# First block of a routed expert layer: order of its downs and place of its counting and weight loads

## The chip, the core and the metric

The kernel runs on one core of a Trainium2 chip. The metric is the device time of one execution in microseconds (us); it is given as the median of several runs.

PE is TensorE (matmul), PEld its weight load, DVE VectorE, ACT ScalarE, POOL GpSimd and SP SyncE. SPq, ACTq and POOLq are the sequencers of these engines, which wait, branch and issue DMAs.

## What is computed

Attention over keys and values that are pooled by eight, then a layer of eight experts of which each token takes one (4608 tokens of 512 numbers, 1024 hidden columns):

```python
k_p = k.reshape(B, H, Sp, pool, D).mean(axis=3)
v_p = v.reshape(B, H, Sp, pool, D).mean(axis=3)
...
x = np.ascontiguousarray(attn_out.transpose(0, 2, 1, 3)).reshape(B * S, H * D)
...
logits = x @ w_gate
expert_idx = np.argmax(logits, axis=1)
...
    h = np.maximum(x_sorted[lo:hi] @ w1[e], 0.0)
    y_sorted[lo:hi] = h @ w2[e]
y = y_sorted[inv_perm]
return (gate_w[:, None] * y).astype(np.float32)
```

## The kernel before

The attention runs as 36 units (NU = 36) of 128 tokens in a loop that is unrolled when the program is built. Its tokens are routed in seven groups. A token's row goes to the tensor in DRAM named x_by_expert, sorted by expert, with an indirect DMA that POOL issues, one for each unit (scatter, L709). The expert layer then takes blocks of 256 sorted tokens. Every fp32 operand is used as a pair of fp16 numbers, high and low, so that each product is three matmuls.

The loop over blocks (For_i, L1316) runs 21 times. The **first block** of expert 0 stands ahead of it, unrolled, and overlaps the last units and the last routing. Its work on PE is eight "ups", f = 0 to 7 (L1007 to L1009, 12 matmuls each), and four "downs" (finish(0, j, half), L1084, 12 matmuls each): j is the half of the tokens, half is the half of the hidden columns. Three of the ups stand inside units 33 to 35 (UPAT), and the rest behind the units. The ups' results lie in four PSUM tiles of two columns f each; relu_hi(k) on ACT (L1075) and relu_lo(k) on DVE (L1078) turn tile k into the high and low fp16 operands of the downs. So downs with half = 0 need k = 0 and 1, and downs with half = 1 need k = 2 and 3. In the trace the downs of j = 1 write the tile pq, those of j = 0 the tile po.

Between the ups two steps of the routing are put:

- counted() (L1104) multiplies the counts per expert (c16) by ones on PE, and rank() runs the ranks of the last group. DVE makes from it the comparison lt and the counts, and SP issues two DMAs of zero rows (L1117).
- ended() (L1138) sums lt on PE, runs the rest of the last group's routing on DVE, and has POOL issue the scatters that are left and three DMAs of zero rows (L1122).

DVE then works out a table of the blocks (table(), L1156 to L1182, 27 small operations). tables() turns it on PE (L1185), DVE writes it as integers into tabs (L1186), and SP reads from tabs which rows the next blocks need. It then issues load_x(1) into the tile qt (L1231) and load_x(2) into vb. The block of iteration 0 is expert 0's second: its rows xT come by a DMA transpose (trans, L929) that SP issues after split_lo (L918), and arrive() (L933) copies them on DVE after tabs. POOL splits the rows of load_x(1) (split_early, L911 and L912), passes their identities on, and enters the loop. In iteration 0 ACT splits x (L915) and then, with DVE, the weights of expert 1 into fp16 pairs (part(), L116 on ACT and L118 on DVE). PE's next block waits for that.

The weights of expert 1 come as four loads of 1 MB from DRAM (wload, L102), all issued by SP, in the units that W1AT names: two halves of w1 at units 28 and 31, then the second half of w2 at unit 32 and the first half at unit 35. A place of NU + k in W1AT would move a load to wlate(k), which issues it behind the units; before the change no load is there.

The engines take their instructions in the order in which the program is written. There is no scheduler between.

Of the kernel before, what the change touches and what calls it, by code (L numbers as in the profile page):

```python
# [22 lines left out]
CW = 73  # L23
WARM = 80
CS = 78
W1AT = (28, 31, 35, 32)
UPAT = (33, 34, 35)
HS = (0, 1, 3, 5, 5)
SLOTS = ((0, 2), (0, 3), (0, 3), (0, 3), (2, 3))
# [3 lines left out]
def kernel(  # L33
# [10 lines left out]
    nc = tc.nc  # L44
# [43 lines left out]
            src = src[e:e + 1] if isinstance(e, int) else src[ds(e, 1)]  # L88
            nc.sync.dma_start(dst, src.rearrange("e p c f -> p (e c) f"))

    def wload(e, i, stage=0):

        lo, hi = (i, i + 1) if isinstance(i, int) else i
        a, n = lo % 4, hi - lo
        s1, s2 = ST[stage]
        if lo < 4:
            src, dst = w1d, s1[a // 2][:, a % 2:a % 2 + n, :]
        else:
            src, dst = w2d, s2[a // 2][:, 2 * (a % 2):2 * (a % 2 + n), :]
            a, n = 2 * a, 2 * n  # L100
        src = src[e:e + 1, :, a:a + n, :] if isinstance(e, int) else src[ds(e, 1), :, a:a + n, :]
        nc.sync.dma_start(dst, src.rearrange("e p c f -> p (e c) f"))  # L102

    last_pool = []

# [120 lines left out]
    def row(x):  # L226

        return x[..., 0:ID].rearrange("p j (h x) -> p j h x", x=HW)[..., 0:D]

    def col(h):  # L230
        return h.rearrange("p j (h x) -> p j h x", x=D)
# [36 lines left out]
    for c in range(5):  # L268
        src = w_gate.rearrange("(h d) e -> d h e", d=D)[:, HS[c]:HS[c] + 3, :]
# [489 lines left out]
    def pooled(n, b):  # L759
        KVS[n, b] = work.tile([128, 5, D], F32, name=n, bufs=2)  # L760
        return kv[(2 * b + (n == "vp")) % 3], KVS[n, b]
# [11 lines left out]
    src, vp = pooled("vp", 0)  # L773
# [86 lines left out]
    for g in range(NPAIR):  # L860
        u0 = 9 * g
        e, o = 2 * g, 2 * g + 1
# [51 lines left out]
    def split_hi():  # L914
        nc.scalar.activation(col(xh[:, :, 0]), row(xg), AF.Copy)  # L915
# [57 lines left out]

    for j, at in enumerate(W1AT):
        if at < NU:
# [26 lines left out]
    def up(s, f, n):  # L1002
        dst = pH[f // 2][:, (f % 2) * BLK:(f % 2) * BLK + n]
        c = slice(f * 128, (f + 1) * 128)
        for d in range(DC):
            wh, wl = W1[s][0][:, d, c], W1[s][1][:, d, c]
            nc.tensor.matmul(dst, wh, xT[:, d, 0:n], start=(d == 0), stop=False)  # L1007
            nc.tensor.matmul(dst, wh, xT[:, DC + d, 0:n], start=False, stop=False)  # L1008
            nc.tensor.matmul(dst, wl, xT[:, d, 0:n], start=False, stop=(d == DC - 1))  # L1009
# [58 lines left out]
    def pair(x, k, n):  # L1068
        return x[:, 2 * k:2 * k + 2, 0:n]

    def ups_of(k, n):
        return pH[k].rearrange("p (f t) -> p f t", f=2)[:, :, 0:n]

    def relu_hi(k, n=BLK):
        nc.scalar.activation(pair(hT[0], k, n), ups_of(k, n), AF.Relu)  # L1075
# [26 lines left out]
    def counted():  # L1102
        pc = pq["pc"] = psA.tile([128, 512], F32, name="pq", bufs=2)
        nc.tensor.matmul(pc[:, 0:E], ones, c16, start=True, stop=True)  # L1104
        rank()
        lt = pq["lt"] = work.tile([128, E], F16, name="lt")
        V.tensor_tensor(lt, pc[:, 0:E], thr, op=OP.is_gt)
        V.tensor_copy(pads, pc[0:1, 0:E])
        for x in range(2):
            h = slice(64 * x, 64 * x + 64)  # L1110
            V.tensor_scalar(padi[h], pc[h, 0:E].rearrange("p (c x) -> p c x", x=2)[:, :, x], pio[h], None, op0=OP.add)
        pcs = pq["pcs"] = work.tile([128, E], F32, name="pcs")
        V.tensor_copy(pcs, pc[:, 0:E])
        for e in range(n0 + n1):
            eng, et = ((nc.sync, ENG.SP), (nc.scalar, ENG.Activation))[e >= n0]
            r = nc.values_load(pads[0:1, e:e + 1], engines=[et], min_val=e * SEG, max_val=e * SEG + SEG - 128)
            padded.append((e, sent(eng.dma_start(xs[ds(r, 64), :], zpad[0:64]))))  # L1117
# [16 lines left out]
    def ended():  # L1134
        pe = psA.tile([128, 512], F32, name="pq", bufs=2)
        end = pq["end"] = pe[:, 0:E]
        for j in range(E):
            nc.tensor.matmul(end[:, j:E], ones, pq["lt"][:, 0:E - j], start=(j == 0), stop=False,  # L1138
                             skip_group_check=True)
        for f in back:  # L1140
            f()
        scatters()
        flush()
        pad_rest()

    def wlate(k):
        for j, at in enumerate(W1AT):
            if at == NU + k:
                wload(1, (2 * j, 2 * j + 2))

    def table():
        end, pcs = pq["end"], pq["pcs"]
# [31 lines left out]
    def tables(pt):  # L1184
        nc.tensor.transpose(pt[0:NK, 0:128], tf[:, 0:NK], ident)  # L1185
        V.tensor_copy(tabs, pt[0:NK, 0:NT])  # L1186
# [3 lines left out]
    for f in range(FC):  # L1190
        if f >= len(UPAT):
            up(0, f, BLK)
        if f + 1 == 5:
            counted()
        if f + 1 == 6:
            ended()
        if f in (1, 3):
            relu_hi(f // 2)
    split_hi()
    for k in (2, 3):  # L1200
        relu_hi(k)
# [10 lines left out]
    W2[1] = [x.rearrange("p (c f) -> p c f", c=FC) for x in views[2:]]  # L1212
    pY.append(psA.tile([128, 512], F32, name="pq", bufs=2))
    pH[3] = psA.tile([128, 512], F32, name="pq", bufs=2)
    for j, half in ((1, 0), (1, 1), (0, 0), (0, 1)):
        if (j, half) == (0, 1):
            tables(pH[3])
            arrive()
        finish(0, j, half)
# [39 lines left out]
        given.append(st)  # L1259

    load_x(1, xg2)
    wlate(1)
    with tc.If(ok2 < 1):
        load_x(0)
        split_x()
# [100 lines left out]
```

## Time and profile before

| what | value |
|---|---|
| time, median of 3 runs | 610.75 us (606.24, 610.75, 615.33) |
| the profiled execution's own time | 615.37 us |
| its span in the profile | 613.4 us |
| PE busy | 570.7 us, 93% of the span |
| DVE, ACT, POOL busy | 51%, 48%, 44% of the span |
| granted TensorE clock, mean | 0.989 of full speed |

Times in the rows below count from the start of the span, which is 613.4 us; 2 us of the execution's own time lie around it. Units and routing end at about 190 us, the first block at about 209 us, and the loop fills the rest. A row's bracket gives the idle time of the engine before it and what ended it; "remote" is a semaphore event to which the profile finds no instruction, and "issue" is a wait to which it finds none.

### The profile page before, as it was taken

The numbers are of one execution on the slowest core, as the hardware profiler recorded it, in microseconds if no ns is written. First come the engines' busy times: TensorE is split into PE (matmuls) and PEld (weight loads), VectorE is DVE, ScalarE is ACT, GpSimd is POOL, SyncE is SP. The second block draws the span as 40 slices with busy tenths as digits, with TensorE's granted clock in tenths as the row PEclk, the third lists the DMA queues.
The fourth block names the chain that finished last, engine by engine and source line by source line (L and its number), as shares of the span: only waits on it lengthen the run. The fifth ranks groups of instructions, "written<-read, shape, count | busy, mean of one in ns | idle before, by whom it ended". The sixth has DMA issues, their size and how long they took to land.

```text
span 613.4 us, 15789 instructions
## 1 busy us (share of the span) xinstructions
PE 570.7 (93%) x4725; PEld 419.2 (68%) x4726; DVE 312.0 (51%) x625; ACT 291.6 (48%) x648; POOL 269.3 (44%) x524
## 2 busy tenths in 40 slices
PE   7888889999887998988999999999999999999995
PEld 6777879887765556645767756767656667567663
DVE  6677897987865355125762782213622471122122
ACT  2677789899941154125653672223522452222122
POOL 5799598997976243211432321122311132211212
PEclk9899999999989899999999999999999999999998
DMA  8997898885496557963986779143332324321200
GB/s 236 315 316 228 264 311 252 277 255 197 137 352 162 166 92 262 380 102 95 309 273 201 205 240 336 56 107 81 78 90 51 86 57 107 96 46 54 68 17 32
DMA packets 96323, 107.15 MB, mean 175 GB/s; under 512 B 54430, under 2 KB 64670, under 8 KB 96288
## 3 DMA queue, kind: packets, MB, share of 16 engines
q1 hardware_dynamic: 89648, 85.72, 49.3%
q0 software_dynamic: 6640, 20.99, 9.2%
q8 instruction: 19, 0.31, 0.2%
q14 instruction: 16, 0.13, 0.1%
HBM read 72.99 MB, written 23.37 MB: 157 GB/s over the span
## 4 chain that ended last, share of the span: by engine, by line
PE 59%; ACT 2%; issue 2%; ACTq 1%; POOLq 0%; DVE 0%; POOL 0%; DVEq 0%
PE po L1084 16%; PE pq L1084 13%; PE ps L1009 5%; PE ps L1007 5%; PE ps L1008 5%; PE pq L1008 3%; PE pp L1008 3%; PE pq L1009 2%; PE pp L1009 2%; PE pq L1007 2%; PE pp L1007 2%; ACT kv L116 1%; ACTq L1223 0%; ACT qt L116 0%; ACT w L116 0%
## 5 line engine op out<-in xcount | busy, mean ns | idle before, releaser
L1084 PEld LDWEIGHTS <-bd 128*128 128x128 f16 x936 | 91.3, 98 | 110.7 <-issue 6.0
L1253 POOL TENSOR_TENSOR spacer<-ql,iG 1x1 f32<-1x1 f32 x44 | 20.3, 462 | 199.1 <-ACT ql L1249 194.1
L1078 DVE SCALAR_TENSOR_TENSOR bd<-ps,bd 128x512 f16<-128x512 f32 (+1 forms) x44 | 27.6, 630 | 157.4 <-ACT bd L1075 145.5
L516 ACT ACTIVATE both<-ps,nmx 128x72 f32<-128x72 f32 x288 | 68.5, 327 | 10.4 <-DVE nmx L509 8.2
L1084 PE MATMUL po<-w,bd 128*128 128x512 f16 x264 | 58.9, 379 | 0.0
L1084 PE MATMUL po<-kv,bd 128*128 128x512 f16 x264 | 58.8, 379 | 0.0
L1075 ACT ACTIVATE bd<-ps 128x512 f16<-128x512 f32 (+1 forms) x44 | 24.0, 547 | 70.5 <-PE L1007 33.4
L1254 POOL DMA_INDIRECT out_dram<-ql,iG x44 | 46.2, 1050 | 21.4 <-issue 20.3
L499 PE MATMUL ps<-bd,qT 128*128 128x144 f32 x256 | 45.2, 300 | 3.3 <-ACT both L516 1.8
L1084 PE MATMUL pq<-kv,bd 128*128 128x512 f16 x216 | 48.1, 379 | 0.0
L1084 PE MATMUL pq<-w,bd 128*128 128x512 f16 x192 | 45.0, 389 | 2.8 <-issue 2.6
L1007 PE MATMUL ps<-kv,qt 128*128 128x256 f16 (+1 forms) x176 | 44.9, 263 | 2.2 <-issue 2.2
L1009 PE MATMUL ps<-kv,qt 128*128 128x256 f16 (+1 forms) x176 | 44.8, 263 | 2.1 <-DVE qt L118 2.1
L1007 PE MATMUL ps<-kv,w 128*128 128x256 f16 (+1 forms) x176 | 43.4, 260 | 1.9 <-ACT kv L116 1.8
L1008 PE MATMUL ps<-kv,qt 128*128 128x256 f16 (+1 forms) x176 | 44.9, 263 | 0.0
L1009 PE MATMUL ps<-kv,w 128*128 128x256 f16 (+1 forms) x176 | 43.3, 259 | 1.6 <-DVE w L118 1.6
L709 POOL DMA_INDIRECT x_by_expert<-both,rpos x36 | 36.5, 1014 | 16.3 <-issue 5.9
L1008 PE MATMUL ps<-kv,w 128*128 128x256 f16 (+1 forms) x176 | 43.4, 260 | 0.0
L1249 ACT ACTIVATE ql<-po,gB 128x512 f32<-128x512 f32 x22 | 15.0, 684 | 57.7 <-PE L1007 33.8
L1007 PEld LDWEIGHTS <-qt 128*128 128x128 f16 x352 | 34.4, 98 | 8.0 <-issue 2.6
L1009 PEld LDWEIGHTS <-qt 128*128 128x128 f16 x352 | 34.4, 98 | 7.0 <-issue 3.2
L1007 PEld LDWEIGHTS <-w 128*128 128x128 f16 x352 | 34.6, 98 | 6.6 <-ACT kv L116 2.2
(252 smaller groups left out, 1357.9 us busy)
## 6 DMA issues: line engine op xcount, KB each, us to landing
both<-in_moe_w_dram SPq DMA_DIRECT2D x6, 2048.0 KB, 11.4
st<-in_moe_w_dram SPq DMA_DIRECT2D x6, 2048.0 KB, 14.6
vb<-x_by_expert SPq DMA_DIRECT2D x16, 578.0 KB
st<-in_moe_w_dram SPq DMA_DIRECT2D x8, 1024.0 KB, 6.1
kv<-in_k_dram SPq DMA_DIRECT2D x7, 1024.0 KB
kv<-in_v_dram SPq DMA_DIRECT2D x7, 1024.0 KB, 10.0
qt<-in_q_dram SPq DMA_DIRECT2D x6, 1024.0 KB
qt<-in_q_dram SPq DMA_DIRECT2D x4, 512.0 KB
```

The costliest lines, as they stand in the source:

```text
L499: nc.tensor.matmul(ps[:, x * 2 * KP:(x + 1) * 2 * KP], t[:, h, :], BD[b % 3][:, :, h, :], start=True, stop=True)
L516: nc.scalar.activation(p[:, h * KP:(h + 1) * KP], ps[:, x * KP:(x + 1) * KP], AF.Exp, bias=nmx[:, x:x + 1], scale=-1.0)
L709: st = nc.gpsimd.indirect_dma_start(out=xs, out_offset=bass.IndirectOffsetOnAxis(ap=Z["pos"][:, u:u + 1], axis=0), in_=X[:, u, :], in_offs ...
L1007: nc.tensor.matmul(dst, wh, xT[:, d, 0:n], start=(d == 0), stop=False)
L1008: nc.tensor.matmul(dst, wh, xT[:, DC + d, 0:n], start=False, stop=False)
L1009: nc.tensor.matmul(dst, wl, xT[:, d, 0:n], start=False, stop=(d == DC - 1))
L1075: nc.scalar.activation(pair(hT[0], k, n), ups_of(k, n), AF.Relu)
L1078: V.scalar_tensor_tensor(pair(hT[1], k, n), ups_of(k, n), 0.0, pair(hT[0], k, n), op0=OP.max, op1=OP.subtract)
L1084: nc.tensor.matmul(y, hT[x][:, f, 128 * j:128 * j + 128], W2[s][z][:, f, :], start=(half == x == z == f == 0), stop=(half == z == 1 and f ...
L1249: nc.scalar.activation(ys[j], pY[j], AF.Copy, scale=gB[:, j:j + 1])
L1253: nc.gpsimd.tensor_tensor(spacer[:, 0:1], ys[j][0:1, 0:1], iG[0:1, j:j + 1].bitcast(F32), op=OP.add)
L1254: st = nc.gpsimd.indirect_dma_start(out=out, out_offset=bass.IndirectOffsetOnAxis(ap=iG[:, j:j + 1], axis=0), in_=ys[j], in_offset=None, b ...
```

## The change

Four edits, all around the first block:

- W1AT moves the two loads of w2 of expert 1 from units 32 and 35 to NU + 0 and NU + 1. wload takes the issuing engine as an argument, and wlate issues on ACT instead of SP. wlate(0) stands ahead of the first block's rest as before. wlate(1) is moved from behind load_x(1) to behind relu_hi(1).
- The order of the loads changes: the first half of w2 goes first, the second half next.
- counted() and ended() each go one up later, behind f = 5 and f = 6.
- The four downs go as (j, half) = (1, 0), (0, 0), (1, 1), (0, 1) instead of (1, 0), (1, 1), (0, 0), (0, 1). tables() and arrive() stay ahead of the last.

```diff
-W1AT = (28, 31, 35, 32)
+W1AT = (28, 31, 36, 37)
...
-    def wload(e, i, stage=0):
+    def wload(e, i, stage=0, eng=None):
...
-        nc.sync.dma_start(dst, src.rearrange("e p c f -> p (e c) f"))
+        (eng or nc.sync).dma_start(dst, src.rearrange("e p c f -> p (e c) f"))
...
-                wload(1, (2 * j, 2 * j + 2))
+                wload(1, (2 * j, 2 * j + 2), 0, nc.scalar)
...
-        if f + 1 == 5:
+        if f + 1 == 6:
             counted()
-        if f + 1 == 6:
+        if f + 1 == 7:
             ended()
         if f in (1, 3):
             relu_hi(f // 2)
+        if f == 3:
+            wlate(1)
...
-    for j, half in ((1, 0), (1, 1), (0, 0), (0, 1)):
+    for j, half in ((1, 0), (0, 0), (1, 1), (0, 1)):
...
     load_x(1, xg2)
-    wlate(1)
```

On ACT, between the last exponential of the routing (rex) and the end of the first block, the order is this (st is the staging tile of w2, bd are the high and low operands, vb holds the rows of block 1):

```order
 L644 ACTIVATE rex<-ra 128x16
+L102 DMA st_65<-in_moe_w_dram 128x4x512
 L1189 TENSOR_LOAD ok2i
 L1075 ACTIVATE bd_158<-ps 128x512 x2
+L102 DMA st_65<-in_moe_w_dram 128x4x512
 L915 ACTIVATE bd_160<-vb_163 128x2x512
 L1075 ACTIVATE bd_158<-pp 128x512 x2
```

Two DMA issues have come in, one ahead of relu_hi(0) and relu_hi(1) and one between these and the split of x.

On SP, at unit 35, the second of the two loads stood between the load of block 1's rows and the reading of ok2i:

```order
 L961 DMA vb_163<-x_by_expert 128x2x578
 L960 UNCONDITIONAL_BRANCH x2
-L102 DMA st_65<-in_moe_w_dram 128x4x512
 L1189 TENSOR_LOAD ok2i
 L1189 ISA x2
```

It has gone from SP, as has the one of unit 32.

On PE, after the twelve matmuls of the down (1, 0) into pq (their last rows are the first ones here), twelve into po have come in:

```order
 L1084 MATMUL pq<-w_00_62,bd_159 128x512
 L1084 LDWEIGHTS bd_158
+L1084 MATMUL po<-w_00_62,bd_158 128x512
+L1084 LDWEIGHTS bd_158
+L1084 MATMUL po<-w_00_62,bd_158 128x512
```

They read bd_158 and bd_159 of the columns f = 0 to 3, which is the down (0, 0); before, the down (1, 1) with f = 4 to 7 stood here.

## Rows read from the trace of the kernel before

**Rows 1.** Timeline of PE in the first block (start, us, engine, line, tiles, count)

```profile
187.91 0.27 PE L1009 MATMUL pp<-kv,w 128*128 128x256 f16 x1
189.25 0.18 PE L1104 MATMUL pq<-c,ones 128*128 128x8 f16 x1 [1.06 <-DVE c L1097]
...
193.38 0.27 PE L1009 MATMUL pp<-kv,w 128*128 128x256 f16 x1
...
195.50 1.24 PE L1084 MATMUL pq<-w,bd 128*128 128x512 f16 x5 [0.16 <-issue]
199.23 4.69 PE L1084 MATMUL pq<-w,bd 128*128 128x512 f16 x12 [2.48 <-issue]
...
206.34 0.27 PE L1185 MATMUL pq<-ident,tf 128*8 128x128 f32 x1
206.45 2.75 PE L1084 MATMUL po<-w,bd 128*128 128x512 f16 x12
```

**Rows 2.** Timeline of ACT around the first block's relus

```profile
177.50 0.70 ACT L528 ACTIVATE ph<-pp 128x640 f16<-128x640 f32 x1 [2.94 <-remote]
...
188.41 1.08 ACT L1075 ACTIVATE bd<-ps 128x512 f16<-128x512 f32 x2 [0.35 <-DVE rm L648]
189.38 1.06 ACT L915 ACTIVATE bd<-vb 128x1024 f16<-128x1024 f32 x1
198.57 1.08 ACT L1075 ACTIVATE bd<-pp 128x512 f16<-128x512 f32 x2 [8.13 <-remote]
```

**Rows 3.** Timeline of DVE: relu_lo, the table's last operation, tabs, arrive

```profile
192.11 1.29 DVE L1078 SCALAR_TENSOR_TENSOR bd<-ps,bd 128x512 f16<-128x512 f32 x2
...
199.69 1.29 DVE L1078 SCALAR_TENSOR_TENSOR bd<-pp,bd 128x512 f16<-128x512 f32 x2 [5.17 <-issue]
...
203.86 0.14 DVE L1182 TENSOR_TENSOR tab<-pq,okf 1x1 int32<-1x1 f32 x1
206.65 0.20 DVE L1186 CAST tabs<-pq 8x48 int32<-8x48 f32 x1 [2.65 <-PE pq L1185]
206.78 0.67 DVE L933 COPY kv<-kv 128x2048 f16<-128x2048 f16 x1
```

**Rows 4.** Timeline of SP's queue: weight loads, transpose, load_x(1)

```profile
166.31 1.10 SPq L102 DMA_DIRECT2D st<-in_moe_w_dram  x2
...
174.20 0.37 SPq L102 DMA_DIRECT2D st<-in_moe_w_dram  x1
...
194.56 3.52 SPq L929 DMA_TRANSPOSE kv<-bd  x1
208.83 0.43 SPq L1231 DMA_DIRECT2D qt<-x_by_expert  x1
```

**Rows 5.** From load_x(1) to the next block: POOL, ACT, PE

```profile
212.98 1.03 POOL L911 TENSOR_TENSOR bd<-qt,zf 128x512 f16<-128x512 f32 x1 [6.38 <-DMA qt<-x_by_expert]
...
224.42 3.88 ACT L116 ACTIVATE qt<-st 128x1024 f16<-128x1024 f32 x4
...
232.12 0.27 PE L1007 MATMUL ps<-kv,w 128*128 128x256 f16 x1 [1.78 <-ACT kv L116]
```

**Rows 6.** Stretches: us; busy of PE, PEld, DVE, ACT, POOL; clock; DMA share; GB/s

```profile
178.00:184.00 6.00, 4.78 (x37) 3.87 (x37) 4.66 (x15) 1.14 (x3) 4.13 (x12) 0.72 0.96 359
...
188.00:194.00 6.00, 4.93 (x53) 4.11 (x52) 4.67 (x22) 2.09 (x4) 4.87 (x9) 1.00 0.55 176
194.00:200.00 6.00, 3.34 (x15) 0.88 (x13) 0.83 (x2) 1.08 (x2) 5.12 (x9) 1.00 0.97 189
200.00:204.00 4.00, 3.88 (x12) 1.27 (x11) 3.79 (x29) 0.05 (x1) 0.67 (x2) 0.57 0.91 327
204.00:209.00 5.00, 5.00 (x25) 2.21 (x23) 0.80 (x2) 0.64 (x1) 1.19 (x2) 1.00 0.15 56
```

**Rows 7.** DMA issues of 188 to 200 us: the transpose, us to landing

```profile
kv<-bd SPq DMA_TRANSPOSE x1, 8.2
```

**Rows 8.** Timeline of POOL: the last scatter

```profile
195.68 0.97 POOL L709 DMA_INDIRECT x_by_expert<-both,rpos  x1 [0.21 <-issue]
```

## Prediction

> **What bounds the kernel now.** I read the page first: PE is busy in 93% of the span, so what counts is where PE waits, and whether the wait is in a chain that all later work hangs on. The timeline of the first block, engine by engine, then shows one such place, and the chain of waits behind it shows how far it reaches.
>
> On PE [rows 1] the reader is to see three things. PE idles 1.06 us ahead of the counting at 189.25, for DVE's cast c. It ends the ups at 193.38 + 0.27 = 193.65 and the down (1, 0) at 195.50 + 1.24 = 196.74. Then it idles 2.48 us and runs the down (1, 1) from 199.23 to 203.92. These 12 matmuls take 4.69 us, where the same 12 take 2.75 us at 206.45. In the 4 us from 200 the mean granted clock is 0.57 [rows 6], so most of that down ran at the lower of the clock's two levels, 1.2 GHz, right behind the idle time.
>
> PE idles there since the down (1, 1) needs relu_hi(2), which ACT begins at 198.57 after 8.13 us of idle time that something "remote" ended [rows 2]. The ups were done at 193.65, so 4.9 us of this wait are not explained by any instruction. DVE's relu_lo(2) and (3) follow at 199.69, end at 200.98, and the table behind them ends at 203.86 + 0.14 = 204.00 [rows 3]. But PE turns the table only at 206.34, because in its order the down (0, 0) stands ahead. From there it is one chain: tabs at 206.65 [rows 3], load_x(1) at 208.83 [rows 4], its rows on POOL at 212.98, the weights of expert 1 on ACT from 224.42, and PE's next block at 232.12, which waited 1.78 us for them [rows 5]. PE itself had 1.78 us to spare there. So what the first block gives is read from the time of tabs, and PE's own gain is only worth something beyond that slack.
>
> **The change, part by part.**
>
> *Downs by halves.* Nothing is added or removed: the same 48 matmuls. The down (0, 0) needs only relu 0 and 1, of which the low part ends on DVE at 192.11 + 1.29 = 193.40 [rows 3]. So it can run right behind (1, 0), from 196.74 for some 2.7 us, into the time in which PE idled 2.48 us. Then (1, 1) starts at about 199.5 instead of 199.23, and needs relu_lo at 200.98 for its last matmuls. At full clock it ends near 202.2. The table is then turned as soon as DVE has it, at 204.0 and no longer at 206.34: **2.3 us earlier**. DVE's table is now late, no longer PE; PE waits some 1.8 us for it. The last down behind it ends at 204.1 + 2.75 = 206.9 instead of 209.2 if the clock holds, and at most at about its old time if that wait brings the clock down as the 2.48 us did (4.69 instead of 2.75 us). Even then the chain through tabs keeps its gain up to PE's 1.78 us of slack. So this part is worth 1.8 to 2.3 us; I take 2.3, since the clock stood at 1.00 until 200 despite the idle 1.06 us and shorter gaps [rows 1, 6].
>
> *Counting one up later.* Between 189.25 and 193.65 PE does three ups and the two small steps, some 1.4 us for an up [rows 1]. With f = 5 ahead of the counting, PE works through the 1.06 us that it idled. Counting still comes at about 189.3, for c is ready then; ended() stands one up behind it as before, so scatters and zero rows are issued as before. The ups end 1.06 us earlier. That is worth nothing if relu_hi(2) still starts at 198.57, and 1.06 us if what is remote keeps its distance from the last up. I take nothing, since the wait outlasts the ups by 4.9 us, and keep 1.06 for the range.
>
> *Two loads out of the units.* SP issues one of the two at 166.31 and the other at 174.20, some 0.4 to 0.55 us each of a queue that has nothing urgent behind it [rows 4]. Without them 2 MB leave the stretch up to 184, where DMA is busy 0.96 of the time [rows 6]. There ACT waits 2.94 us for something remote at 177.50 [rows 2], and from 178 to 184 the clock is 0.72. If the full DMA engines cause that wait, it goes: a gain of up to 2.9 us. If not, nothing. I take nothing: the longer wait of the same name, 8.13 us at 198.57, began at 190.44, and in 188 to 194 DMA was busy only 0.55 with no weight load in it.
>
> *Two loads into the block.* On ACT each costs one issue, 0.37 to 0.55 us by SP's rows [rows 4]. The first stands ahead of relu_hi(0), which moves from 188.41 to about 188.9, the second ahead of the split of x, which then ends near 191.4 instead of 190.44 [rows 2]. DVE takes both up only at 192.11 and behind 193.40 [rows 3], so this is hidden. Their waits (POOL's split of the old contents) ended long before. On the DMA engines the 2.1 MB take 5.8 us at the 359 GB/s of 178 to 184. From 188 to 204 the engines are free for 6 x 0.45 + 6 x 0.03 + 4 x 0.09 = 3.2 us [rows 6]. So 2.6 us of work go over 204, into a stretch that was 0.15 busy: all is done near 207. What could be late are the transpose of block 1's rows, which landed at 194.56 + 8.2 = 202.8 [rows 4, 7] and now lands between 202.8 and 208.6, and the last scatter, issued at 195.68 [rows 8], for which load_x(1) waits. PE needs xT at 206.9 and has 1.78 us in hand; load_x(1) would be issued at 206.5. I put the cost at nothing, with up to 2.3 us, the whole gain, as its bound. The weights themselves are needed at 224.42, long after.
>
> The Trainium skill speaks against this part: its page "DMA: Bandwidth & Descriptors", section "Issuing engines are not separate DMA queues", says that DMAs issued from several engines run on the same 16 DMA engines and interleave, and that another issuer saves only the time of issuing. By that rule the loads on ACT get no lane of their own, and scatters and transpose share with them; the trace before shows no load issued by ACT. It is the second case below.
>
> **The sum.** 0 for the loads, 0 for the counting, -2.3 for the downs. Against the profiled execution, 615.37 us, that is 613.1; that execution is 4.6 us above the median of the runs, 610.75, and the gain carries over as a difference: **608.5 us**.
>
> **How it could go otherwise.**
>
> - *Forecast, chance 0.5:* tabs 2 to 3 us earlier, everything behind shifted by it: 608.5, with 607 to 610 as its own range.
> - *The loads eat it, 0.2:* transpose or scatters late by 2.3 us, so that load_x(1) or xT stands where it stood. For it: DMA is busy 0.97 and 0.91 in the block already. Against it: PE's slack and the empty 204 to 209. 610.75.
> - *More than forecast, 0.15:* the remote waits go with the loads (2.9 us) and with the earlier end of the ups (1.06 us): 610.75 - 2.3 - 2.9 - 1.06 = 604.5. For it: a full DMA share around 177.50; against it: the wait at 198.57 without weight loads.
> - *Slower, 0.15:* the remote wait ahead of relu_hi(2) grows with the traffic in the block. It decides once relu_hi(2) starts later than 198.57 + 2.3 = 200.9. If it grows by the whole 5.8 us of the loads, the table is done at 209.8, 3.5 us after 206.34: 614.3. For it: this wait stands amid POOL's scatters and the transpose; against it: a weight load was never near it.
>
> The range runs from 604 to 614: it takes in the first two cases, most of the others, and is about that of the three runs before (606.24 to 615.33), which differ by more than the forecast. About 2% (12 us) is what a measurement of this kernel can surely tell from no change. No case reaches that: faster 0.03, same 0.95, slower 0.02, the small ones for something unseen.
>
> **What would show it.** Right: no idle time of PE between the downs (1, 0) and (0, 0), the table turned on PE directly behind DVE's last operation of it, tabs near 204.5, the next block's first matmul near 230 and no wait of load_x(1) or arrive for a DMA. Wrong: relu_hi(2) after 200.9; SP waiting for scatters after tabs; arrive waiting for the transpose beyond 207; ACT late with relu_hi(0) behind its DMA issue; or PE's next block held by something else, so that 2.3 us at tabs don't come out at 232.12.

## The result and the profile after

The changed kernel takes 616.83 us in the median (614.76 to 618.80, 6 runs), against 610.34 us before (606.24 to 615.33, 6 runs): a ratio of 1.0108, 95% interval 1.0067 to 1.0149. The prediction was 608.5 us with a range up to 614. The change is within 2%, but the sign is wrong: it costs about 6.5 us where 2.3 us of gain were forecast. The profiled execution takes 617.48 us, its span is 615.6 us. All ratios in this document leave out executions that a slower state of the chip disturbed; the medians don't.

All that the change was said to do at the front of the block is there, and more. On ACT both waits that something remote had ended [rows 2] are gone (a second profile of the kernel before, in group one, lacks them too, so the change need not be the reason); relu_hi(2) starts at 188.78 instead of 198.57:

```profile
175.69 0.70 ACT L528 ACTIVATE ph<-pp 128x640 f16<-128x640 f32 x1 [1.20 <-PE pp L523]
...
188.78 1.09 ACT L1075 ACTIVATE bd<-pp 128x512 f16<-128x512 f32 x2 [1.52 <-PE pp L1009]
```

The timeline of PE of the changed kernel shows downs without a gap, the table turned at 196.35 instead of 206.34 [rows 1], and then idle time of 11.34 us where there was none:

```profile
193.76 2.75 PE L1084 MATMUL pq<-w,bd 128*128 128x512 f16 x12
196.35 0.27 PE L1185 MATMUL pq<-ident,tf 128*8 128x128 f32 x1
196.46 2.75 PE L1084 MATMUL po<-w,bd 128*128 128x512 f16 x12
210.55 0.37 PE L1007 MATMUL ps<-kv,w 128*128 128x256 f16 x1 [11.34 <-DVEq L1317]
...
234.18 0.27 PE L1007 MATMUL ps<-kv,w 128*128 128x256 f16 x1 [1.18 <-DVE kv L118]
```

DVE, in the same kernel, tells what PE waits for: tabs is written 10 us earlier than before [rows 3], and then arrive waits 11.85 us for the transpose:

```profile
196.66 0.20 DVE L1186 CAST tabs<-pq 8x48 int32<-8x48 f32 x1 [1.26 <-PE pq L1185]
208.70 0.69 DVE L933 COPY kv<-kv 128x2048 f16<-128x2048 f16 x1 [11.85 <-DMA kv<-bd]
```

SP's queue (timeline of the changed kernel) was held by the issue of the transpose for 8.99 us, where it was 3.52 [rows 4], and load_x(1), 9.7 us behind tabs instead of 2.2, stood at 206.34:

```profile
190.88 8.99 SPq L929 DMA_TRANSPOSE kv<-bd  x1
206.34 0.43 SPq L1233 DMA_DIRECT2D qt<-x_by_expert  x1
```

Of these 9.7 us SP spent 4.5 waiting for POOL's zero rows (waits of SP's queue: us in total, times, longest):

```profile
SPq L1233 <- DMA x_by_expert<-zpad,padi: 4.5, 1, 4.5
```

The DMA issues of the changed kernel from 184 to 199 us (count, KB each, median us to landing), and the transpose of 190.88 by itself:

```profile
st<-in_moe_w_dram ACTq DMA_DIRECT2D x2, 1024.0 KB, 10.3
x_by_expert<-zpad SPq DMA_DIRECT2D x2, 144.5 KB, 8.0
x_by_expert<-both,rpos POOLq DMA_INDIRECT x6, 8.2
x_by_expert<-zpad,padi POOLq DMA_INDIRECT x3, 11.9
...
kv<-bd SPq DMA_TRANSPOSE x1, 17.7
```

The transpose lands after 17.7 us instead of 8.2 [rows 7]. The stretches of the changed kernel (us; busy of PE, PEld, DVE, ACT, POOL; clock; DMA share; GB/s) show the price twice. The DMA engines are full up to 208, and move ever less from 192 on. Behind 200 no weight load moves any more:

```profile
192.00:196.00 4.00, 4.00 (x20) 1.85 (x19) 3.15 (x28) 0.00 (x0) 3.34 (x7) 1.00 1.09 396
196.00:200.00 4.00, 3.21 (x16) 1.28 (x14) 0.20 (x1) 1.38 (x2) 2.21 (x4) 1.00 1.04 253
200.00:204.00 4.00, 0.00 (x0) 0.00 (x0) 0.00 (x0) 0.00 (x0) 0.00 (x0) 0.91 1.20 218
204.00:208.00 4.00, 0.00 (x0) 0.00 (x0) 0.00 (x0) 0.00 (x0) 0.00 (x0) 0.50 1.08 131
208.00:212.00 4.00, 1.45 (x8) 1.03 (x9) 0.69 (x1) 0.00 (x0) 1.45 (x2) 0.50 0.59 169
```

In 200 to 208 no compute engine does anything. Behind it PE starts at half clock (0.50): from its first matmul at 210.55 to the first relu on ACT at 214.99 it needs 4.4 us. In the second profile of the kernel before, at full clock, the same stretch takes 3.0 us (201.83 to 204.81). So the clock takes some 1.4 us more. The weights of expert 1 are split on ACT from 224.45, and PE's next block starts at 234.18. Before it was 224.42 and 232.12 [rows 5], in an execution that had lost time earlier: against that one PE's next block is only 2.1 us late.

### The profile page after: what moved, and what is told of

It reads as the page before. It is cut to its first block, busy times and chain, and to the rows that moved or that the text cites. A ratio compares the mean times of both kernels' runs of the same rounds, so it can differ in the third digit from the quotient of the medians.

```text
span 615.6 us, 15786 instructions
## 1 busy us (share of the span) xinstructions
PE 568.4 (92%) x4725; PEld 420.2 (68%) x4726; DVE 311.6 (51%) x625; ACT 292.0 (47%) x648; POOL 268.6 (44%) x524
## 5 line engine op out<-in xcount | busy, mean ns | idle before, releaser
L1007 PE MATMUL ps<-kv,w 128*128 128x256 f16 (+1 forms) x176 | 43.7, 262 | 12.5 <-DVEq L1317 11.3
L1007 PE MATMUL ps<-kv,qt 128*128 128x256 f16 (+1 forms) x176 | 45.9, 267 | 2.4 <-issue 2.4
L1009 PE MATMUL ps<-kv,qt 128*128 128x256 f16 (+1 forms) x176 | 45.8, 266 | 1.6 <-DVE qt L118 1.6
L1007 PEld LDWEIGHTS <-w 128*128 128x128 f16 x352 | 34.7, 99 | 17.4 <-issue 11.8
L1008 PE MATMUL ps<-kv,qt 128*128 128x256 f16 (+1 forms) x176 | 46.0, 268 | 0.0
L1084 PE MATMUL pq<-w,bd 128*128 128x512 f16 x192 | 42.9, 379 | 0.0
L1007 PEld LDWEIGHTS <-qt 128*128 128x128 f16 x352 | 34.7, 99 | 7.9 <-issue 2.9
L1009 PEld LDWEIGHTS <-qt 128*128 128x128 f16 x352 | 34.7, 99 | 6.0 <-issue 2.5
## 6 DMA issues: line engine op xcount, KB each, us to landing
both<-in_moe_w_dram SPq DMA_DIRECT2D x6, 2048.0 KB, 10.9
qt<-in_q_dram SPq DMA_DIRECT2D x6, 1024.0 KB, 10.9
```

Of the source, the lines that this page charges most:

```text
L1084: nc.tensor.matmul(y, hT[x][:, f, 128 * j:128 * j + 128], W2[s][z][:, f, :], start=(half == x == z == f == 0), stop=(half == z == 1 and f ...
```

## The experiments

Each ratio is to the kernel before on the same chip, with its 95% interval in brackets. The five groups ran on four chips; groups two and five had the same one. Later line numbers shift by up to three with the edits.

### Group one: the parts of the change, and the kernel before again

**Downs and counting alone.** The changed kernel with both loads back in units 32 and 35:

```diff
-W1AT = (28, 31, 36, 37)
+W1AT = (28, 31, 35, 32)
```

> The change without its loads: downs by halves and the counting one up later, both loads of w2 of expert 1 issued by SP in units 32 and 35 as before. Theory (the two loads inside the block are the loss: they push the scatters, the zero rows and the transpose of block 1's rows): the transpose lands about 8 us after its issue as before, arrive and load_x(1) wait for no DMA, tabs come 2 to 3 us earlier than before and the time is 607 to 609 us, below both kernels. Rival (the new order itself is the loss: the earlier table only meets scatters that are as late as ever, or the downs cost what they save): 613 to 617 us, with SP's long wait for the zero rows and PE's long idle time still there.

Measured: 609.3 us, 0.9966 (0.9927 to 1.0005). The transpose landed after 7.0 us, arrive stood at 198.15, after 1.11 us of waiting for it, and load_x(1) at 199.72. The loss is gone; the interval takes in 1, so a gain is not shown.

**Loads alone.** The kernel before, with the loads moved:

```diff
-W1AT = (28, 31, 35, 32)
+W1AT = (28, 31, 36, 37)
...
-                wload(1, (2 * j, 2 * j + 2))
+                wload(1, (2 * j, 2 * j + 2), 0, nc.scalar)
...
+        if f == 3:
+            wlate(1)
```

> The other part alone: only the two loads are moved into the block and issued by ACT; downs and counting stand as before. Theory (the loads are the loss): units and ups end some 5 us earlier as in the changed kernel, without the waits that something remote ended, but the transpose takes over 15 us from issue to landing and the zero rows land near 206; arrive and load_x(1) wait for them, and the time is 614 to 620 us. Rival (the loss needs the new order): about 610 us or less, with the transpose landing near 8 us after its issue.

Measured: 620.44 us, 1.0140 (1.0088 to 1.0193). The transpose landed after 16.1 us. SP's queue and DVE of this kernel read as in the changed one:

```profile
192.69 9.04 SPq L929 DMA_TRANSPOSE kv<-bd  x1
204.03 0.43 SPq L1233 DMA_DIRECT2D qt<-x_by_expert  x1
```
```profile
208.90 0.69 DVE L933 COPY kv<-kv 128x2048 f16<-128x2048 f16 x1 [9.06 <-DMA kv<-bd]
```

These two runs settle which part loses. The loads alone cost 1.4%, and without them there is no loss. Whether it is their time, their queue or their absence from the units is settled in groups two to four.

**The kernel before once more.**

> The kernel before once more, for a second profile of it. Theory (the waits on something remote near 177 and 198 follow from the full DMA engines in the units and are there in every execution): they are there again with 1 to 8 us each, and the time is 606 to 615 us. Rival (they belong to that one execution, the slowest of those measured): they are absent or under 1 us, and the profiled execution is below 611 us.

Measured: 611.78 us, 0.9999 (0.9958 to 1.0039); its profiled execution took 611.82 us, where the one that the prediction was made from took 615.37. It has neither of the two remote waits. Its ACT and its DVE:

```profile
190.41 1.08 ACT L1075 ACTIVATE bd<-pp 128x512 f16<-128x512 f32 x2 [3.25 <-PE pp L1009]
```
```profile
198.30 0.20 DVE L1186 CAST tabs<-pq 8x48 int32<-8x48 f32 x1 [2.40 <-PE pq L1185]
199.99 0.69 DVE L933 COPY kv<-kv 128x2048 f16<-128x2048 f16 x1 [1.49 <-DMA kv<-bd]
```

Its PE, at the start of the loop's first block and of the next one, and its ACT, at the first relu of the loop:

```profile
201.83 0.27 PE L1007 MATMUL ps<-kv,w 128*128 128x256 f16 x1 [0.98 <-DVEq L1316]
...
224.71 0.27 PE L1007 MATMUL ps<-kv,w 128*128 128x256 f16 x1 [1.88 <-ACT kv L116]
```
```profile
204.81 0.60 ACT L1075 ACTIVATE bd<-ps 128x512 f16<-128x512 f32 x1 [3.24 <-PE L1007]
```

Here relu_hi(2) stands at 190.41, tabs at 198.30 and not at 206.65, and arrive already waits 1.49 us for the transpose. In this execution the front of the block has next to no spare time: all that PE has in hand are the 1.88 us that its next block waits for ACT. That block starts at 224.71, 7.4 us earlier than in the first profile (232.12 [rows 5]) and 9.6 us earlier than with the loads alone on the same chip (234.30; 234.18 in the changed kernel). So the cover that the prediction counted on lay in the remote waits. The rival held as to the waits (the time, 611.82, lies just above its 611): the 8 us wait is no fixed part of the kernel. It is not a thing of one execution either, as group two shows.

**Loads late.** The changed kernel with both loads on SP behind load_x(2):

```diff
-                wload(1, (2 * j, 2 * j + 2), 0, nc.scalar)
+                wload(1, (2 * j, 2 * j + 2), 0, nc.sync)
...
-    wlate(0)
     ok2 = nc.values_load(ok2i[0:1, 0:1], engines=[ENG.Activation, ENG.DVE, ENG.Pool, ENG.SP], min_val=0, max_val=1)
...
-        if f == 3:
-            wlate(1)
...
     load_x(2)
+    wlate(0)
+    wlate(1)
```

> The changed kernel with both loads issued by SP behind load_x(1) and load_x(2), after scatters, zero rows and transpose. Theory: the units go without the remote waits (tabs near 197 as in the changed kernel), the transpose lands 8 us or less after its issue, load_x(1) is issued as soon as the zero rows are there, some 5 us ahead of the kernel before, and the loads land before their use near 220: 603 to 607 us. Rival (transpose and zero rows are late for their own traffic, not for the loads): arrive still waits to about 206 and the time is 610 us or more. Second rival (loads so late that the weights are): PE's next block waits for the splitting of the weights, which waits for the loads; 610 us or more with ACT or DVE waiting for DMA there.

Measured: 613.93 us, 1.0036 (0.9999 to 1.0072). The theory missed: the transpose landed only after 12.5 us although no load was near it, arrive waited to 204.55, as the rival had it. So transpose and scatters can hold each other up without any load.

### Group two: when, how much, and the transpose by itself

On this chip the kernel before took 616.57 us, and remote waits were back, in each of the six profiles taken there (four here, two in group five), in different sizes and not always both of them. Neither the kernel before nor the changed one was profiled on it. As an example, ACT in the first run of this group:

```profile
196.66 1.09 ACT L1075 ACTIVATE bd<-pp 128x512 f16<-128x512 f32 x2 [8.16 <-remote]
```

With relu_hi(2) that late, the front has spare time, and what the DMA engines do behind it counts for less. These runs are read with that in mind.

**Loads later still**, behind the transpose of the following block's rows:

```diff
     trans()
+    wlate(0)
+    wlate(1)
     with tc.If(ok2 < 1):
```

> As the run with late loads, but both loads are issued by SP still later, behind load_x(1), load_x(2) and the transpose of the following block's rows, so near 213 instead of 207.6. They are needed by the splitting of w2 near 224 to 228. Theory (late loads cost 4.6 us against the kernel with the loads in the units, since they met that transpose and load_x(2)): the following transpose is held under 2.5 us and lands under 5.5 us after its issue, and the time is 607 to 610 us. Rival (the late loads had no part in it; the first transpose is slow without any load, as in that run, where it ended 9.15 us after its issue): 612 to 616 us again, with arrive waiting to about 204. Second rival (the loads are now too late): idle time of ACT or DVE for the DMA into st near 228.

Measured: 617.48 us, 1.0011 (0.9977 to 1.0044). arrive followed tabs at once (202.68 behind 202.55). Neither theory nor rivals came out as stated. The kernel is level with the one before; whether it would gain elsewhere stays open.

**One load** in the block:

```diff
-W1AT = (28, 31, 36, 37)
+W1AT = (28, 31, 36, 32)
```

> The changed kernel with only the first of the two loads inside the block (1 MB on ACT ahead of relu_hi(0)); the other one is issued by SP in unit 32. Theory (the loss follows the bytes that meet scatters and transpose): about half of it, arrive near 203 and load_x(1) near 203, 611 to 614 us. Rival (it is the second load, issued just ahead of the transpose, that does the harm): within 1 us of the kernel with no load in the block, 608 to 610 us. Second rival (any load there is enough): 616 to 618 us.

Measured: 617.23 us, 1.0004 (0.9974 to 1.0034); transpose 11.7 us, arrive at 206.57, 3.32 us of waiting for it. Inconclusive: relu_hi(2) stood at 197.17 behind a remote wait of 6.08 us, which can have covered what one load does.

**Loads by SP** at the same places in the program:

```diff
-                wload(1, (2 * j, 2 * j + 2), 0, nc.scalar)
+                wload(1, (2 * j, 2 * j + 2), 0, nc.sync)
```

> The changed kernel with its two loads issued by SP at the same places in the program, so in the queue of the transpose and ahead of it. Theory (the traffic counts, not the issuer): the transpose again ends over 12 us after the place where SP took it up, and the time is within 2 us of the changed kernel, 615 to 619 us. Rival (ACT's own queue is what lets the loads push in between transpose and scatters): in one queue the loads go first, the transpose then runs in some 6 us, arrive is near 202 and the time is 609 to 613 us.

Measured: 615.93 us, 0.9969 (0.9933 to 1.0006). The loss is gone, but the trace gives a reason that neither theory had: SP issued the loads from 177.17 on, ACT in the changed kernel at 184.17 and 185.27. SP has no work of the block in front of it, so the same line of the program ran 7 us earlier (9 us in group three, 175.09 against 184.06). Group four separates the two.

**Transpose late**, behind load_x(1), with the loads in the units:

```diff
-    trans()
     for k in (2, 3):
         relu_lo(k)
...
             tables(pH[3])
-            arrive()
...
     load_x(1, xg2)
+    trans()
+    arrive()
```

> The kernel with the new downs and counting and no load in the block, but the transpose of block 1's rows is moved behind load_x(1), so that it meets no scatter. Theory (transpose and scatters hold each other up): the zero rows land earlier, load_x(1) is issued at about 198 instead of 199.72, the transpose then ends within 5 us of its issue, arrive is near 205, PE idles some 6 us, and the time is 612 to 616 us. Rival (they don't disturb each other): load_x(1) stays at 199.5 or later.

Measured: 625.41 us, 1.0125 (1.0074 to 1.0177). PE idled 9.04 us, arrive stood at 213.63. That a late transpose costs PE directly is shown. The other half is not: load_x(1) went at 205.90, since tabs was late here (203.89), and the transpose, issued at 206.77 behind the scatters, needed more than the 5 us of the theory: arrive, which waited for it, came 6.9 us later.

### Group three: the changed kernel and its nearest relatives on one chip

**The changed kernel again**, with no edit.

> The changed kernel unchanged, beside its variants on one chip. Theory (its two loads run from 184 to 198, amid scatters, zero rows and transpose, and all of these land late): as in its first profile the transpose ends over 14 us after its issue and load_x(1) is issued near 206; 1.0 to 1.5% above the kernel before where that one has no wait on something remote behind the ups, and about level with it (within 0.5%) on a chip where that wait is there anyway, as in the second group of runs. Rival (the first profile was an odd execution): level with the kernel before in both cases.

Measured: 616.22 us, 1.0103 (1.0059 to 1.0148); the median alone is 0.6% above the 612.64 us of the kernel before. Transpose 16.1 us, arrive at 207.01. load_x(1) went at 201.64 here, but landed only for POOL's split at 209.30, 7.7 us later (4.1 us before, 208.83 to 212.98 [rows 4, 5]): in SP's queue it stood behind the transpose, which was still running.

**Downs and counting again**, as in group one.

> New downs and counting, both loads in the units as before, beside the changed kernel on one chip. Theory (the two loads inside the block are the whole loss): 6 to 9 us below the changed kernel and 1 to 3 us below the kernel before, where the remote wait is absent. Rival (chip against chip made the difference): within 3 us of the changed kernel.

Measured: 613.6 us, 1.0014 (0.9981 to 1.0046). The theory's 6 to 9 us below the changed kernel came out as 2.6 us of medians, and as 5.5 us by the ratios (0.0089 x 612.64). It is level with the kernel before, not 1 to 3 us below it. The transpose landed after 12.7 us this time (7.0 in group one), with no load beside it.

**Loads by SP again.**

> The changed kernel with the loads issued by SP: SP came to them at 177.2, 7 us ahead of ACT, so that they had landed by 190, ahead of the transpose. Theory (what counts is when the loads run, not on which queue): level with the kernel that has the loads in its units, so 5 to 9 us below the changed kernel; transpose done within 8 us of its issue. Rival (any load outside the units costs): 1% above the kernel before, as the changed kernel.

Measured: 609.43 us, 0.9948 (0.9918 to 0.9978); transpose 8.1 us.

**Only the order of the downs.** The kernel before with

```diff
-    for j, half in ((1, 0), (1, 1), (0, 0), (0, 1)):
+    for j, half in ((1, 0), (0, 0), (1, 1), (0, 1)):
```

> The kernel before with only the order of the downs changed. Theory (tabs come earlier by the turn of the table, but load_x(1) then waits for the zero rows, which POOL and the DMA engines finish no earlier): tabs 1 to 2.5 us earlier than before and load_x(1) at most 1 us earlier; 0 to 2 us below the kernel before. Rival (the gain at tabs carries over whole, as forecast): 2 to 3 us below it, with no wait of SP for zero rows between tabs and load_x(1).

Measured: 611.7 us, 0.9994 (0.9954 to 1.0034). The median is 0.9 us lower, but no gain is measured, and tabs did not come earlier (12.3 us behind the counting at 186.69, as in the kernel before once more, 198.30 behind 185.97). PE and DVE of this run show why:

```profile
190.93 2.75 PE L1084 MATMUL pq<-w,bd 128*128 128x512 f16 x12
193.52 2.75 PE L1084 MATMUL po<-w,bd 128*128 128x512 f16 x12
196.11 2.75 PE L1084 MATMUL pq<-w,bd 128*128 128x512 f16 x12
198.70 0.27 PE L1185 MATMUL pq<-ident,tf 128*8 128x128 f32 x1
```
```profile
199.01 0.20 DVE L1186 CAST tabs<-pq 8x48 int32<-8x48 f32 x1 [2.36 <-PE pq L1185]
```

In either order three downs stand ahead of the table. Where none of them has to wait, the order changes nothing; DVE still waits 2.36 us for PE.

### Group four: time or issuer, and what an earlier transpose is worth

**Loads by ACT, but in unit 34**, where SP would issue them:

```diff
+        else:
+            put(34, "act", wload, 1, (2 * j, 2 * j + 2), 0, nc.scalar)
...
-    wlate(0)
```

(wlate(1) is gone as well.)

> The changed kernel with both loads still issued by ACT and on ACT's queue, but in unit 34, at about 176 instead of 184.2 and 185.2, near where SP issues them in the run with SP. Theory (the time of the loads decides, not who issues them): they have landed by 192, the transpose ends within 8 us of its issue, and the time is 5 to 9 us below the changed kernel, as with SP. Rival (a second queue beside SP's slows the transpose whenever it runs): transpose still over 10 us, time within 3 us of the changed kernel.

Measured: 607.87 us, 1.0008 (0.9982 to 1.0033); transpose 8.2 us, arrive at 200.92. ACT's queue:

```profile
175.91 1.15 ACTq L102 DMA_DIRECT2D st<-in_moe_w_dram  x2
```

From ACT's own queue, 8 to 9 us earlier, the loads cost nothing. The time counts, not the issuer. The Trainium skill says in "DMA: Bandwidth & Descriptors", section "Issuing engines are not separate DMA queues", that DMAs of all issuers interleave on the same 16 engines. These runs agree: early loads measure 1.0008 from ACT and 0.9948 to 0.9995 from SP.

**Earlier transpose.** In the next three kernels the split of block 1's rows and the transpose stand ahead of the counting:

```diff
+    split_hi()
+    split_lo()
+    trans()
     for f in range(FC):
...
-    split_hi()
     for k in (2, 3):
         relu_hi(k)
     for k in (0, 1):
         relu_lo(k)
-    split_lo()
-    trans()
```

With the loads where the change has them:

> The changed kernel, loads where it has them, but block 1's rows are split and the transpose issued ahead of the counting (at about 187 instead of 190.9). Theory (the transpose that starts among scatters and loads is what PE waits for): it meets fewer of them, ends near 196 to 199, PE's idle time of 10 us shrinks to 1 to 4 us; what is left is load_x(1), whose zero rows still land near 202 to 205: 610 to 614 us. Rival (with the loads in the block any transpose takes 14 us or more): it ends at 201 or later, 614 us or more. The price: the routing behind the split on DVE is 0.8 to 1.3 us later.

Measured: 616.93 us, 1.0136 (1.0102 to 1.0169). The rival held. Issued at 189.42, the transpose met loads and scatters from the start, held SP's queue for 13.03 us and landed after 20.6; SP's zero rows stood behind it, and load_x(1) went at 210.65.

With the loads in the units:

> Both loads in the units, new downs and counting, and the earlier split and transpose. Theory (on top of the loads, transpose and scatters hold each other up, 5.7 to 9.4 us for a transpose that alone ends 3.85 us after its issue): the transpose is done near 193, arrive follows tabs at once, near 197.5, PE doesn't idle, and load_x(1) is issued at 199 to 200: 606 to 609 us, below every other kernel here. Rival (the later routing costs what the transpose gives): level with the kernel with the loads in the units, 610 to 613 us.

Measured: 606.71 us, 0.9982 (0.9954 to 1.0009). Transpose 7.1 us; arrive followed tabs at once (197.46 behind 197.33), load_x(1) went at 199.80 without a wait for a DMA. The time lies where the theory had it, but the kernel before takes 608.54 us on this chip, and the interval includes 1: PE doesn't wait for its rows, but then for the weights of expert 1 (next block at 222.54 [1.52 <-ACT kv L116]), whose splitting hangs on load_x(1).

With the loads by SP, now behind the transpose in its queue:

> The changed kernel with loads by SP, and the earlier split and transpose. In SP's queue the transpose now stands ahead of the loads where those are still to be issued. Theory: as the run with SP, 0.5% below the kernel before, and up to 2 us less where the transpose no longer meets the last scatters. Rival (the transpose at 187 meets the loads, which end near 190): transpose over 8 us and no gain over the run with SP.

Measured: 614.16 us, 1.0097 (1.0064 to 1.0131). I had expected a gain. SP's queue and its waits:

```profile
187.16 2.60 SPq L929 DMA_TRANSPOSE kv<-bd  x1
189.87 2.62 SPq L102 DMA_DIRECT2D st<-in_moe_w_dram  x2
194.55 2.31 SPq L1117 DMA_DIRECT2D x_by_expert<-zpad  x2
207.47 0.42 SPq L1233 DMA_DIRECT2D qt<-x_by_expert  x1
```
```profile
SPq L1233 <- DMA x_by_expert<-zpad: 4.3, 2, 4.0
SPq L1233 <- DMA x_by_expert<-zpad,padi: 2.4, 1, 2.4
```

The transpose was early, and arrive stood at 197.59, directly behind tabs at 197.46. But the loads ran from 190 on, the zero rows behind them landed late, and load_x(1) waited 6.7 us for these. It went 7.7 us later than with the loads in the units (199.80), and ACT's splitting is late by as much (223.46 against 215.81). PE then waits 3.41 us for it and takes the next block up at half clock (0.50 in 226 to 230):

```profile
224.56 0.39 PE L1007 MATMUL ps<-kv,w 128*128 128x256 f16 x1 [3.41 <-ACT qt L116]
```

So the loads in the block cost 1% by way of the zero rows, even where PE has its first rows in time.

### Group five: the zero rows, and SP's loads a third time

**Zero rows of experts 2 and 3 by ACT**, on top of the earlier transpose with the loads in the units:

```diff
-    n0, n1 = 2, 0
+    n0, n1 = 2, 2
```

> Loads in the units, new downs and counting, earlier split and transpose, and in addition the zero rows of experts 2 and 3 no longer come from POOL's first indirect DMA behind its last scatter, but from two plain DMAs that ACT issues right behind the counting, in the 2.9 us that it idles ahead of relu_hi(2). load_x(1) needs the zero rows up to expert 2 only. Theory (with PE's wait for the transpose gone, the zero rows behind POOL's scatters bind the front: there load_x(1) stood at 199.8, 2.5 us behind tabs): load_x(1) goes at 197.5 to 198.5, 1 to 2 us earlier, and the time is 1 to 3 us below the kernel before, some 0.3 to 0.5%. Rival (the scatters themselves are as late as the zero rows): load_x(1) within 0.5 us of 199.8 and no gain. Second rival: ACT's two issues push relu_hi(2) and with it the table back by more than 1 us.

Measured: 612.0 us, 0.9967 (0.9937 to 0.9996), on the chip with the remote waits. load_x(1) waited 0.2 us for a DMA, but it went only at 204.09, since tabs stood at 200.75: the unit's wait of 2.88 us (remote) on ACT had put the counting back to 188.59. The stated time of load_x(1) was missed, the gain was met, at its lower end. Of all kernels run this and the loads by SP on one chip are the only ones whose interval ends below 1; among 19 intervals one such can come by chance, and the loads by SP didn't come out so on two other occasions.

**Loads by SP, third time.**

> The changed kernel with the loads by SP once more, on the chip of the run beside it. Theory: 0.3 to 0.5% below the kernel before, as on two chips so far (0.9969 and 0.9948), with the transpose done within 8 us. Rival: that gain was chance, level with the kernel before (0.998 to 1.002), as the run with ACT in unit 34.

Measured: 613.54 us, 0.9995 (0.9962 to 1.0028). Over three groups, 0.9969, 0.9948 and 0.9995: level with the kernel before or a little faster, and 1% better than with the issue by ACT. A sure gain it is not.

### One figure for all of them

From the counting on PE (L1104) to the first splitting of expert 1's weights on ACT (L116), worked out as the difference of the two starts. Groups two and five are left out, and before's first profile too, for their remote waits. Each figure is of one execution: the same kernel with the loads in the units has 29.9 and 34.7.

| kernel | transpose to landing, us | counting to splitting, us | ratio |
|---|---|---|---|
| loads in the units, group one | 7.0 | 215.75 - 185.84 = 29.9 | 0.9966 |
| earlier transpose, loads in the units | 7.1 | 215.81 - 185.87 = 29.9 | 0.9982 |
| before, once more | 8.6 | 216.58 - 185.97 = 30.6 | 0.9999 |
| loads by ACT in unit 34 | 8.2 | 216.88 - 185.84 = 31.0 | 1.0008 |
| loads by SP, group three | 8.1 | 218.77 - 186.94 = 31.8 | 0.9948 |
| order of downs only | 11.6 | 219.44 - 186.69 = 32.8 | 0.9994 |
| loads in the units, group three | 12.7 | 219.95 - 185.26 = 34.7 | 1.0014 |
| loads late | 12.5 | 222.16 - 186.68 = 35.5 | 1.0036 |
| loads alone | 16.1 | 224.47 - 187.32 = 37.2 | 1.0140 |
| earlier transpose, loads by SP | landed before 197.5 | 223.46 - 186.07 = 37.4 | 1.0097 |
| the changed kernel, group three | 16.1 | 223.03 - 185.55 = 37.5 | 1.0103 |
| earlier transpose, loads by ACT | 20.6 | 226.04 - 188.33 = 37.7 | 1.0136 |
| the changed kernel, first profile | 17.7 | 224.45 - 185.66 = 38.8 | 1.0108 |

All kernels of this table with both loads in the block need over 37 us and lose 1.0 to 1.4%; all others stay below 36 and within 0.6% of the kernel before.

## Why the prediction was wrong

**What bounds the kernel.** Right in its chain (tabs, load_x(1), splitting, next block), wrong in its size. The 4.9 us of relu_hi(2)'s wait that no instruction explained were taken as a part of the kernel. The second profile of the kernel before has no such wait, and tabs stands there at 198.30. So the first step of the prediction that failed is the sentence that the gain "carries over as a difference" from an execution 4.6 us above the median: gain and cover rested on the wait of that execution. With it the next block started at 232.12, without it at 224.71. That the 4.6 us are this wait is likely, but not shown.

**Downs by halves, -2.3 us.** It failed: alone they measure 0.9994. The new order has as many downs ahead of the table as the old; it can gain only where the down (1, 1) has to wait, as it did behind the remote wait. That it gains there is argued from the first profile; the order alone was not run on a chip with that wait. Turning the table ahead of the down (1, 1) was not tried.

**Counting one up later, 0.** The idle 1.06 us ahead of the counting are gone with it (L1104 at 185.84 without idle time in group one), and tabs then comes 11.0 us behind the counting instead of 12.3. In time it is not resolved: with the downs, 0.9966 and 1.0014.

**Loads out of the units, 0.** Right, as far as the runs tell. The remote waits went in the changed kernel's profile, but they are missing too in the kernel before once more and in the four other profiles with the loads in the units outside groups two and five. Loads by ACT in unit 34 and in the units are level.

**Loads into the block, 0, at most 2.3 us.** This is the second step that failed, and it is the loss: 1.4% alone. "I put the cost at nothing" rested on two things.

- The cover: a PE that needs xT at 206.9 and a load_x(1) at 206.5, both late through the stall. Without it the changed kernel's last down ends at 196.46 + 2.75 = 199.2, and SP wants load_x(1) near 199, some 2 us behind tabs. A late transpose then stands on the path nearly whole.
- The size: at most 5.8 us for the transpose, so 8.2 + 5.8 = 14.0 us from issue to landing. It took 17.7, 16.1 and 16.1 us (the changed kernel twice, the loads alone), 7.5 to 9.1 more than the 8.6 of the second profile. The free time of 3.2 us between 188 and 204 was also the stalled execution's. In the second profile only 4 x 0.14 + 4 x 0.16 = 1.2 us are free there:

```profile
188.00:192.00 4.00, 4.00 (x31) 2.82 (x30) 3.52 (x9) 1.08 (x2) 3.55 (x5) 1.00 0.86 262
192.00:196.00 4.00, 4.00 (x20) 1.80 (x19) 3.68 (x29) 0.40 (x1) 3.34 (x8) 1.00 1.02 164
196.00:200.00 4.00, 4.00 (x20) 1.84 (x19) 0.21 (x2) 0.28 (x1) 2.37 (x5) 1.00 1.12 313
200.00:204.00 4.00, 3.02 (x24) 2.16 (x23) 0.68 (x1) 0.69 (x1) 0.00 (x0) 1.00 0.84 230
```

That the points in time came out ("all is done near 207", the transpose "between 202.8 and 208.6"; it landed at 190.88 + 17.7 = 208.6, load_x(1) went at 206.34) is luck: loads and transpose were issued about 4 us earlier than the prediction had them, at 184.17 and 190.88 instead of some 188 and 194.56.

Beside the second profile, on its own chip, the loads alone make arrive 8.9 us later (208.90 against 199.99), and the median 9.0 us longer (620.44 - 611.47). Also the bound of 2.3 us, "the whole gain", was no bound: a wait that takes the place of another one is not limited by it.

**The rivals.** "The loads eat it" had the right cause with that same false bound. "Slower" put the loss at relu_hi(2); it was early, and the loss came behind tabs. "More than forecast" came true for the front (tabs 10 us earlier) and was worth nothing.

**What would show it.** The signs for wrong were well chosen: SP waits for zero rows after tabs, arrive waits for the transpose beyond 207. ACT's issues ahead of relu_hi(0) did no harm, as forecast.

Three things stay open. Why remote waits come on one chip in every profile (2.9 to 10.9 us) and on three others in none; no run changed them on purpose, and the chip of the first two profiles is not on record. Whether the change is level with the kernel before on a chip with these waits, as its expectation in group three says; it was not run there. And what one load in the block costs, since it ran only where these waits can cover it.

## What to carry to other kernels

Before a wait is used as cover or counted as a gain, see that it is there in a second profile, above all when the profiled execution is slower than the median and nothing explains the wait. Bytes that move into a stretch with a transpose and scatters are priced against the earliest moment at which somebody can need what is queued there, and a transpose at its own rate, not at that of plain loads. A DMA's place is its time of issue: the same line on another engine's queue ran 7 to 9 us earlier, and that alone was worth the 1% that the change lost.

## What was not expected of the hardware

- **A transpose among other transfers.** The same transpose of 512 KB landed 7.0 to 12.7 us after its issue beside scatters and zero rows and 16.1 to 20.6 with both weight loads among them (11.7 with one). It also held the queue of SP that issued it, for 2.6 to 5.8 us beside scatters, 8.6 to 13.0 with both loads.
- **A transpose alone fills the DMA engines at a lower rate.** In the loop of the second profile of the kernel before, from 447 to 449 us, nothing but such a transpose moves, in packets of under 512 B. The DMA share is 1.12 at 208 GB/s:

```profile
447.00:449.00 2.00, 2.00 (x11) 0.93 (x10) 0.00 (x0) 0.69 (x1) 0.18 (x1) 1.00 1.12 208
```

Plain loads and scatters together, without a transpose, move 359 GB/s at a share of 0.96 [rows 6]. Shared with others a transpose is dearer still: in 200 to 204 of the changed kernel (queue, packets, MB, share of the engines) q1 is the transpose and q0 the indirect DMAs that POOL had issued:

```profile
q1 hardware_dynamic: 790, 0.20, 51.6%
q0 software_dynamic: 176, 0.65, 65.0%
```

So a price by bytes at 359 GB/s, as in the prediction, is too low for such a stretch.

- **Late release by something remote.** On the chip of groups two and five ACT idled 5.1 to 10.9 us ahead of relu_hi(2) until something remote in five profiles, and 3.9 us until PE's ups in the sixth. On the three others it idled 1.5 to 3.3 us, always until PE's ups. The kernel with the loads by SP ran on both kinds: 10.9 and 5.1 us there, 1.9 here.
